# Chunk-selecting attention and a squared-ReLU feed-forward: the first four head pairs reordered, and their queries loaded in four transfers

## The chip, the cores and the metric

The kernel runs on one core of a Trainium2 chip. The core has a matrix engine (TensorE, PE in the profile, its weight loads PEld), a vector engine (VectorE, DVE), a scalar engine (ScalarE, ACT), a general one (GpSimd, POOL) and SyncE (SP), which here only issues transfers. Each engine works through its own instructions in the order in which they were written; semaphores tie the engines together. Transfers run on 16 DMA engines. The metric is device time in microseconds (us).

## The reference

What is computed, for 4 batches, 8 heads, 768 tokens and head dimension 64, and after it for 3072 tokens of width 512 with a hidden layer of 2048:

```python
k_chunks = k.reshape(B, H, nc, 32, D)
k_min, k_max = k_chunks.min(3), k_chunks.max(3)
ub = sum_d(maximum(q * k_min, q * k_max))        # a bound for each chunk of 32 keys
ub = where(causal, ub, -1e9)
top_chunks = argsort(ub)[..., -6:]
scores = q @ k.T / sqrt(D)
scores = where(chunk is in top_chunks and the key is not later than the query, scores, -1e9)
attn = softmax(scores)
x = (attn @ v)                                   # to B*S rows of H*D
h = relu(x @ w_in)
out = (h * h) @ w_out
```

## The kernel before

**Staging.** The work is cut into 32 slots, each a batch, a half of the sequence (384 queries) and a pair of heads; eight groups of four slots (`ORDER`), `s` counts slots and `NP` is 4. Slots 0 to 3 are the first half of batch 0, pairs 0 to 3. They are the start of the kernel, and the only slots with no feed-forward work beside them; from slot 4 on, units of the feed-forward of earlier groups are taken from a queue and stand between the attention's steps on TensorE.

**The order is written by hand** (`tc.manual_schedule()`): every engine's instructions stand in the order of the Python calls. For one slot these are the steps:

- `step_T` transposes k and q of the pair on TensorE (`tk`, `tq`), one after the other. In slots 0 to 3, q comes from the tile `qn0`, token by token, in three 128x128 transposes; k from the packed tile `kn`, in eight small ones. `step_P` picks the PSUM pools and calls it.
- `relus_T` makes the positive and negative part of q on ACT (`qr`); `extrema` makes chunk minima and maxima of k on DVE (`km`, two reductions) and spreads them (`kbd`). `step_T2` is both. `place` copies `tk` or `tq` to its place in `kqs`, on the engine it is given.
- `step_U` bounds the chunks (`ub`, TensorE), finds the eight largest of each row (`m`, DVE) and marks what is below the sixth; in slots 0 to 3 it writes the marks into columns of `qn0`.
- `step_V` transposes queries and marks together (`qt`) and copies them to `kqs` on DVE (L383; L393 and L394 from slot 4 on).
- `step_E(s, head, bank)` multiplies keys with queries (`ps`, three PSUM buffers) and takes the exponential on ACT (`e`). The one-hot codes of the keys' chunks in `kqs`, written by `codes`, add a large negative number for marked chunks. In bank 1 POOL cuts the diagonal with a select (L416).
- `step_F` multiplies with V (`po`), divides (`r`, `x`). `x_T` and `x_copy` transpose x for the feed-forward, whose first matmul is `ph` (L522).

`busy` issues small matmuls whose result nobody reads; they hold a PSUM buffer of the pool that they are given.

**Loads.** Pairs 0 and 1 of k and q come through `load_staged` on the queues of SP and ACT in float32 and are cast by `step_cast`. All other loads are POOL's, which converts on the way: first k of pairs 2 and 3 (`load_packed("k", 0, 4)`), then six loads of q of those pairs (`load_q0`: one for each block of 128 tokens and each head of a pair), then V (`load_vt`), and then those in `later`, which `go` issues. POOL's transfers use eight semaphores in turn: the ninth, the second of V, waits until the first has landed. SP issues, behind the staged loads, the one-hot codes of pairs 1 to 3 (`codes(0, 0, nc.sync.dma_start, 1, NP)`, L166, two transfers); those of pair 0 are copied by DVE.

**The front** is L618 to L674. In pair 0 and 1 it reads:

```python
    step_cast("k", 1)
    step_V(0)
    step_E(0, 0, 0)
    step_E(0, 0, 1)
    step_cast("q", 1)
    step_P(1)
    step_T2(1)
```

The loop that follows does slot s and prepares slot s + 2 (`step_P(s + 2)`, `relus_T`, `extrema`, L665 to L673), up to slot 5. Slot 4 begins at L698, before the first feed-forward units are pushed (L709). For slot 4, `step_P` uses the PSUM pool of the feed-forward (`ph`, two buffers) for k.

Of the kernel before, what the change touches and what calls it, by code (L numbers as in the profile page):

```python
# [16 lines left out]
HT = 3  # L17
HB = HT * 128
# [21 lines left out]
def kernel(  # L40
# [9 lines left out]
    nc = tc.nc  # L50
    B, H, S, D = q.shape
    NC = S // CH
    NT = S // 128
    NP = H // 2
# [17 lines left out]
    SROW = (0, D)  # L72
# [34 lines left out]
            in_=rows(n, *ORDER[g], 0, H)[:, 128 * j:128 * (j + 1)]  # L107
            .rearrange("h p d -> p h d"))

    def load_q0(j, h):  # L110
        nc.gpsimd.dma_start(
            out=qn0[:, j, 2:NP, 1 + h, :],
            in_=q[0, 4 + h:H:2, 128 * j:128 * (j + 1)].rearrange("h p d -> p h d"))

    def load_v(b, h0, h1):
        nc.gpsimd.dma_start(
# [3 lines left out]
    def load_vt(b, j):  # L120
        nc.gpsimd.dma_start(  # L121
            out=vn[b % 2][:, :, j, 0:D],
            in_=v[b, :, 128 * j:128 * (j + 1)].rearrange("h p d -> p h d"))
# [22 lines left out]
    ident = consts.tile([128, 128], BF16, tag="ident")  # L146
    make_identity(nc, ident)
    load_packed("k", 0, 4)
    for j in range(HT):
        for h in range(2):  # L150
            load_q0(j, h)
    for j in range(HT):
        load_vt(0, j)

    oneh = consts.tile([D, S], BF16, tag="oneh")
    nc.vector.tensor_scalar_mul(
# [3 lines left out]
    def codes(i, half, copy, p0=0, p1=NP):  # L160
        for h in range(2):
            copy(kqs[i][SROW[h]:SROW[h] + D, h, p0:p1, 2 * half, :],
                 oneh[:, HB * half:HB * half + HB].unsqueeze(1)
                 .to_broadcast([D, p1 - p0, HB]))

    codes(0, 0, nc.sync.dma_start, 1, NP)  # L166

    cmask = consts.tile([128, HT, 2, NC], BF16, tag="cmask", name="cmask")
    nc.vector.memset(cmask, 0.0)
# [40 lines left out]
    st = {}  # L210
# [18 lines left out]
    def step_cast(n, p):  # L229
        if n == "k":  # L230
            nc.vector.tensor_copy(packed("k", 0)[:, 2 * p:2 * p + 2], staged["k", p])
        else:
            nc.scalar.copy(qn0[:, :, p, 1:3, :], staged["q", p])

    def step_T(s, kp, qp):

        b, half, p = slots[s]
        t = st.setdefault(s, {})
        for n, (pool, tag) in zip("kq", (kp, qp)):
            x = t[n] = pool.tile([128, HB], BF16, tag=tag, name="t" + n)  # L240
            if n == "q" and s < NP:
                for j in range(HT):
                    nc.tensor.matmul(
                        x[:, 128 * j:128 * (j + 1)],
                        lhsT=qn0[:, j, p, 1:3, :].rearrange("p h d -> p (h d)"),
                        rhs=ident, is_transpose=True, start=True, stop=True)
                continue
            for hh in range(2):
                for j in range(TP):
                    nc.tensor.matmul(  # L250
                        x[D * hh:D * hh + D, PP * j:PP * j + PP],
                        lhsT=packed(n, s // NP)[:, 2 * p + hh, D * j:D * j + D],
                        rhs=ident[0:PP, 0:PP], is_transpose=True, start=True, stop=True)

    def step_T2(s):
        relus_T(s)
        extrema(st[s]["k"], s)
        if s >= NP:
            place(s, "k", nc.vector.tensor_copy)
            place(s, "q", nc.scalar.copy)  # L260

    def relus_T(s):
        b, half, p = slots[s]
        t = st[s]
        qr = t["qr"] = work.tile([128, 2, HB], BF16, tag="qr", bufs=3, name="qr")
        c = 128 * (1 - half)
        for w in range(2):
            o, i = qr[:, w, c:], t["q"][:, c:]
            if s >= NP:
                o, i = by_token(o), in_order(t["q"])[:, c // TP:, :]  # L270
            nc.scalar.activation(o, i, ACT.Relu, scale=(-1.0, 1.0)[w])

    def place(s, n, copy, h0=0, h1=2):
        b, half, p = slots[s]
        for h in range(h0, h1):
            copy(by_token(kqs[b % 2][QROW[h]:QROW[h] + D, h, p, 2 * half + "kq".index(n), :]),  # L276
                 in_order(st[s][n][D * h:D * h + D]))
# [58 lines left out]
    def step_P(s):  # L336
        if s // NP >= ON_PE:
            relus(s)
            return
        step_T(s, *((S_, Y) if s == NP + 1 else (F, Y) if s < NP + 2 else  # L340
                    (Y, S_) if s < 2 * NP + 1 else (S_, A)))
        if s >= NP + 2 and s != 2 * NP + 1:
            step_T2(s)
# [282 lines left out]
    step_P(0)  # L626
    busy(10)
    step_T2(0)
    place(0, "k", nc.scalar.copy)
    blank(1, NP, 3)  # L630
    step_U(0)
    busy(9)
    step_cast("k", 1)
    step_V(0)
    step_E(0, 0, 0)
    step_E(0, 0, 1)
    step_cast("q", 1)
    step_P(1)
    step_T2(1)
    for i in range(3):  # L640
        nc.vector.memset(nsel[i], 0.0)
    early.close()
# [1 line left out]
    for s in range(NP):  # L644
        last = s + 1 == NP
        if s:
            step_E(s, 0, 0)
            step_E(s, 0, 1)
        step_E(s, 1, 0)
        busy(8)  # L650
        step_U(s + 1)
        if last:
            place(s + 1, "k", nc.vector.tensor_copy, 0, 1)
        else:
            place(s + 1, "k", nc.scalar.copy)
        step_E(s, 1, 1)
        if last:
            place(s + 1, "k", nc.scalar.copy, 1, 2)
        if s:
            step_F(s - 1, 0)  # L660
            step_F(s - 1, 1)
        if last:
            x_T(0, 0, F)
        step_V(s + 1)
        step_P(s + 2)  # L665
        if last:
            x_copy(0, 0, 0, 2, nc.vector.tensor_copy)
            busy(10, *F)
        else:
            relus_T(s + 2)  # L670
            if s + 2 == NP:
                place(s + 2, "q", nc.scalar.copy)
            extrema(st[s + 2]["k"], s + 2)  # L673
        go(s, 99)  # L674
    parts = []

# [4 lines left out]
    for s, (b, half, p) in enumerate(slots):  # L681
        if s < NP:
            continue
        hb = s // NP
        nb = len(BANKS[half])
        hf = nb // 2
        quota = [((4, 4, 4, 4) if hb == 1 else (8, 6, 7, 7))[p]]
        for fn, *a in first.get(s, ()):
            fn(*a)
        if ON_PE - 1 <= hb < 2 * B - 1 and p == (2 if hb < ON_PE else 1):  # L690
            parts.extend(step_K(hb + 1))

        def f1():
            if quota[0] and queue:
                quota[0] -= 1
                fill(1, True)

        if s == NP:  # L698
            for n in range(hf):
                step_E(s, 0, n)  # L700
            step_F(s - 1, 0)
            step_F(s - 1, 1)
            relus_T(s + 1)
            x_T(0, 1, F, (0,))
            x_copy(0, 1, 0, 1, nc.vector.tensor_copy)
            busy(8, *A)
            x_T(0, 1, F, (1,))
            x_copy(0, 1, 1, 2, nc.vector.tensor_copy)
            push(0)  # L709
            extrema(st[s + 1]["k"], s + 1)  # L710
            place(s + 1, "k", nc.vector.tensor_copy)
            place(s + 1, "q", nc.scalar.copy)
        if s == 2 * NP:
            for n in range(hf):
                step_E(s, 0, n)
            relus_T(s + 1)
            place(s + 1, "q", nc.scalar.copy)
            x_T(1, 0, A)
            x_copy(1, 0, 0, 2, nc.vector.tensor_copy)
            step_F(s - 1, 0)  # L720
            step_F(s - 1, 1)
            f1()
            f1()
            x_T(1, 1, A)
            x_copy(1, 1, 0, 2, nc.scalar.copy)
            push(1)
            extrema(st[s + 1]["k"], s + 1)
            place(s + 1, "k", nc.vector.tensor_copy)
        if p == 0 and hb > 2:
            step_F(s - 1, 0)  # L730
            step_F(s - 1, 1)
            step_X(hb - 1, False)
        else:
            f1()
        if s > NP and s != 2 * NP:
            for n in range(hf):
                step_E(s, 0, n)
        k1()
        f1()
        if p == 0 and hb > 2:  # L740
            f1()
            f1()
        if hb > 1 and s != 2 * NP:
            f1()
        go(s, 2)
        for n in range(hf, nb):
            step_E(s, 0, n)
        if hb < ON_PE and p:
            k1()
        if s + 1 < NS:  # L750
            step_U(s + 1)
        f1()
        if p and s > NP:
            step_F(s - 1, 0)
            step_F(s - 1, 1)
        if half == 0:
            f1()
        if hb < ON_PE and p:
            k1()
        for n in range(hf):  # L760
            step_E(s, 1, n)
        f1()
        if s + 1 < NS:
            step_V(s + 1)
        k1()
        go(s, 99)
        for n in range(hf, nb):
            step_E(s, 1, n)
        k1()
        if s + 2 < NS:  # L770
            step_P(s + 2)
        f1()
        if half == 0:
            f1()
        while quota[0] and queue:
            f1()
# [38 lines left out]
```

## Time and profile before

| | us |
|---|---|
| median of 3 runs | 279.37 (278.88 to 279.73) |
| profiled execution, whole time | 278.57 |
| its span, first to last instruction | 276.9 |
| TensorE busy | 259.0 (94%) |
| ScalarE busy | 181.9 (66%) |
| VectorE busy | 168.8 (61%) |
| GpSimd busy | 92.1 (33%) |

The granted clock of TensorE is 1.000 over the whole span. A timeline row gives the start in us from the span's start, the length in us, the engine, the line, the operation with the tile it writes and what it reads, how many such instructions follow one another (x), and in brackets the idle time of the engine before it and what ended it. A row with x over 1 holds several instructions, which overlap a little. In the chain of waits a row is a start, a length and what the time went to. A row of the transfers gives the tile, the queue, the number, the size and the us from issue to landing.

### The profile page before, as it was taken

To read this page: it belongs to the slowest core of one execution; us is meant where nothing else is said; L and a number is where in the kernel's file an instruction comes from. 1 tells how busy PE (TensorE), PEld (TensorE's weight loads), DVE (VectorE), ACT (ScalarE), POOL (GpSimd) and SP (SyncE) were. 2 spreads that over 40 slices of the span, in tenths; PEclk is the share of its full clock that TensorE was granted. 3 is DMA by queue.
4 is the path that set the end of the run, shared out by engine and by line. 5 is a ranking of instruction groups with operands and counts; after the bars stand their busy time and mean duration, and the time that the engine had idled before them with its cause. 6 is when DMAs were issued, how large, how long until landed. Compare 5 with 4: busy or idle time off the path is not lost.

```text
span 276.9 us, 6716 instructions
## 1 busy us (share of the span) xinstructions
PE 259.0 (94%) x2497; PEld 163.3 (59%) x2497; DVE 168.8 (61%) x645; ACT 181.9 (66%) x400; POOL 92.1 (33%) x137
## 2 busy tenths in 40 slices
PE   7687898899999999999999999999999999999994
PEld 6466555556666566655565566745565566655543
DVE  6687999656994368635894378616883455413411
ACT  6798889588975787835675777825674777615500
POOL 8796356316532016521551116701121111000000
PEclk9999999999999999999999999999999999999999
DMA  7999999959999249998599459996423200111002
GB/s 132 142 204 212 182 214 208 138 66 139 156 182 146 71 115 151 123 162 151 115 143 129 114 104 141 127 130 163 101 63 59 76 2 0 40 39 40 38 38 76
DMA packets 98272, 32.05 MB, mean 116 GB/s; under 512 B 84640, under 2 KB 93984, under 8 KB 98240
## 3 DMA queue, kind: packets, MB, share of 16 engines
q0 software_dynamic: 64720, 14.42, 61.7%
q1 hardware_dynamic: 32432, 16.88, 28.8%
q10 hardware_dynamic: 1088, 0.33, 0.5%
q8 instruction: 19, 0.31, 0.5%
q14 instruction: 13, 0.11, 0.1%
HBM read 27.26 MB, written 6.29 MB: 121 GB/s over the span
## 4 chain that ended last, share of the span: by engine, by line
PE 68%; DVE 13%; DMA 8%; ACT 5%; issue 2%; POOL 1%; SPq 1%; ACTq 0%; POOLq 0%
PE py L538 25%; PE ph L522 22%; PE ps L407 9%; PE po L432 7%; DMA qn<-in_q_dram 3%; DMA kn<-in_k_dram 3%; DVE h L528 2%; ACT e L412 2%; DVE kq L276 2%; DMA xT<-x 1%; DVE km L319 1%; ACT ht L526 1%; SPq L482 1%; DVE x L442 1%; ACT ob L544 1%
## 5 line engine op out<-in xcount | busy, mean ns | idle before, releaser
L412 ACT ACTIVATE e<-ps 128x512 bf16<-128x512 f32 x192 | 96.8, 550 | 26.6 <-PE ps L407 26.5
L522 PE MATMUL ph<-xT,w_in 128*128 128x384 bf16 x512 | 99.2, 326 | 0.6 <-DMA xT<-x 0.3
L538 PE MATMUL py<-w_out,h 128*128 128x512 bf16 x368 | 88.5, 379 | 1.2 <-ACT ob L544 0.9
L526 ACT ACTIVATE ht<-ph 128x384 bf16<-128x384 f32 x128 | 62.6, 499 | 27.3 <-PE ph L522 25.7
L416 POOL TENSOR_SCALAR_AFFINE_SELECT e<-e 128x384 bf16<-128x384 bf16 x64 | 34.5, 543 | 137.5 <-ACT e L412 137.5
L528 DVE TENSOR_TENSOR h<-ht 128x384 bf16<-128x384 bf16 x128 | 46.3, 374 | 43.5 <-ACT ht L526 43.3
L522 PEld LDWEIGHTS <-w_in 128*128 128x128 bf16 x512 | 47.4, 97 | 30.3 <-issue 1.4
L407 PE MATMUL ps<-kq 128*128 128x384 bf16 (+2 forms) x320 | 56.4, 278 | 2.8 <-ACT e L412 1.2
L538 PEld LDWEIGHTS <-h 128*128 128x128 bf16 x368 | 34.9, 97 | 35.3 <-issue 1.7
L407 PEld LDWEIGHTS <-kq 128*128 128x128 bf16 x320 | 26.3, 97 | 14.4 <-issue 2.6
L432 PEld LDWEIGHTS <-e 128*128 128x128 bf16 x672 | 25.6, 98 | 7.3 <-issue 2.0
L361 DVE MAX8 m<-ub 128x8 f32<-128x24 f32 (+1 forms) x160 | 16.7, 171 | 20.6 <-PE ub L354 19.7
L432 PE MATMUL po<-vn,e 128*128 128x65 bf16 x672 | 26.9, 194 | 1.4 <-POOL e L416 0.8
L544 ACT COPY ob<-py 128x512 f32<-128x512 f32 x19 | 11.1, 585 | 22.7 <-PE py L538 22.3
L442 DVE TENSOR_TENSOR x<-po,r 128x384 bf16<-128x384 f32 x32 | 17.8, 557 | 1.1
L393 DVE COPY kq<-qt 64x384 bf16<-64x384 bf16 (+1 forms) x28 | 8.8, 315 | 12.4 <-PE qt L389 12.4
L105 POOL DMA_DIRECT2D kn<-in_k_dram x15 | 13.3, 888 | 0.2
L105 POOL DMA_DIRECT2D qn<-in_q_dram x15 | 13.3, 886 | 0.0
L319 DVE TENSOR_TENSOR km<-km 128x384 bf16<-128x384 bf16 (+3 forms) x40 | 11.5, 287 | 1.1
L121 POOL DMA_DIRECT2D vn<-in_v_dram x12 | 10.7, 903 | 2.0 <-DVE kq L383 1.5
L354 PE MATMUL ub<-kbd,qr 128*128 128x48 bf16 (+1 forms) x160 | 9.6, 180 | 1.9 <-DVE kbd L218 1.0
L354 PEld LDWEIGHTS <-qr 128*128 128x128 bf16 x160 | 7.7, 96 | 4.2 <-ACT kq L276 1.3
(67 smaller groups left out, 198.8 us busy)
## 6 DMA issues: line engine op xcount, KB each, us to landing
out_dram<-ob SPq DMA_DIRECT2D x23, 256.0 KB, 2.2
kq<-kqT SPq DMA_DIRECT2D x10, 384.0 KB, 5.2
w_in<-in_moe_w_in_dram POOLq DMA_DIRECT2D x2, 1024.0 KB, 13.2
w_out<-in_moe_w_out_dram POOLq DMA_DIRECT2D x2, 1024.0 KB, 18.2
kn<-in_k_dram POOLq DMA_DIRECT2D x15, 128.0 KB, 6.0
qn<-in_q_dram POOLq DMA_DIRECT2D x15, 128.0 KB, 5.9
vn<-in_v_dram POOLq DMA_DIRECT2D x12, 128.0 KB, 9.2
vn<-in_v_dram POOLq DMA_DIRECT2D x4, 384.0 KB, 8.2
```

The source lines that it names most:

```text
L105: nc.gpsimd.dma_start(out=nat_of(n, g)[:, DM * j:DM * j + DM].rearrange("p (h d) -> p h d", d=D), in_=rows(n, *ORDER[g], 0, H)[:, 128 * j: ...
L354: nc.tensor.matmul(ub[:, j - j0], lhsT=st[s]["qr"][:, w, 128 * j:128 * (j + 1)], rhs=kbds[b % 2][:, p, w, :, 0:ncs], start=False, stop=(j ...
L361: nc.vector.max(out=m8[:, j, hh, :], in_=ub[:, j - j0, hh, :])
L407: nc.tensor.matmul(ps[:, at:at + 128 * m], lhsT=kqs[b % 2][:, hh, p, 2 * (j // HT), 128 * (j % HT):128 * (j % HT + 1)], rhs=qc(s, hh)[:, c ...
L412: nc.scalar.activation(e[:, 512 * n + lo:512 * n + hi], ps[:, lo:hi], ACT.Exp, scale=float(scale))
L416: nc.gpsimd.affine_select(out=d, in_=d, compare_op=ALU.is_ge, fill=0.0, base=0, channel_multiplier=-1, pattern=[[0, 3], [1, 128]])
L432: nc.tensor.matmul(po[:, hh, i, :], lhsT=t["e"][hh][:, c:c + 128], rhs=vn[b % 2][:, 2 * p + hh, j, :], start=(j == 0), stop=(j == iq))
L442: nc.vector.tensor_mul(x[:, :, 128 * p:128 * (p + 1)].rearrange("p j (h d) -> p h j d", h=2), po[:, :, :, 0:D], r.to_broadcast([128, 2, HT ...
L522: nc.tensor.matmul(ph[:, 0:HB], lhsT=w_in[:, ki, 128 * f:128 * (f + 1)], rhs=xT[:, ki, :], start=(ki == 0), stop=(ki == NKI - 1))
L526: nc.scalar.activation(ht, ph[:, 0:HB], ACT.Relu)
L528: nc.vector.tensor_mul(h, ht, ht)
L538: nc.tensor.matmul(py[t], lhsT=h2[hb, f][:, 128 * t:128 * (t + 1)], rhs=w_out[:, f, :], start=(f == 0), stop=(f == NFI - 1))
```

## The change

The queries of pairs 2 and 3 are loaded by head, each load with all 384 tokens: heads 4 and 5 before V, heads 6 and 7 after it. The codes of pairs 1 to 3 are issued later in SP's queue: two one-element memsets on DVE, behind the extrema of pair 0, write into the region that the codes then overwrite, so SP waits for them. The cast of pair 1's q stands before pair 0's scores, its k transposes before them, its q transposes after their first bank, its extrema on DVE after its relus are issued. `step_T` gets an argument that selects k or q. Slot 4 is prepared in slot 3, after the scores of its first head, instead of at the end of slot 2, and the copies of its q come after the last exponential of slot 3; slot 5 is prepared in slot 4, after `step_F` of slot 3.

```diff
-    def load_q0(j, h):
+    def load_q0(h):
         nc.gpsimd.dma_start(
-            out=qn0[:, j, 2:NP, 1 + h, :],
-            in_=q[0, 4 + h:H:2, 128 * j:128 * (j + 1)].rearrange("h p d -> p h d"))
+            out=qn0[:, :, h // 2, 1 + h % 2, :],
+            in_=q[0, h, 0:HB].rearrange("(j p) d -> p j d", p=128))
...
     load_packed("k", 0, 4)
-    for j in range(HT):
-        for h in range(2):
-            load_q0(j, h)
+    for h in (4, 5):
+        load_q0(h)
     for j in range(HT):
         load_vt(0, j)
+    for h in (6, 7):
+        load_q0(h)
...
-    codes(0, 0, nc.sync.dma_start, 1, NP)
...
-    def step_T(s, kp, qp):
+    def step_T(s, kp, qp, ns="kq"):
...
-        for n, (pool, tag) in zip("kq", (kp, qp)):
+        for n in ns:
+            pool, tag = kp if n == "k" else qp
...
     step_T2(0)
+    for h in range(2):
+
+        nc.vector.memset(kqs[0][SROW[h]:SROW[h] + D, h, 1, 0, 0:1], 0.0)
+    codes(0, 0, nc.sync.dma_start, 1, NP)
     place(0, "k", nc.scalar.copy)
...
     step_cast("k", 1)
+    step_cast("q", 1)
     step_V(0)
+    step_T(1, F, Y, "k")
     step_E(0, 0, 0)
+    step_T(1, F, Y, "q")
+    relus_T(1)
     step_E(0, 0, 1)
-    step_cast("q", 1)
-    step_P(1)
-    step_T2(1)
+    extrema(st[1]["k"], 1)
...
             step_E(s, 0, 1)
+        if last:
+            step_P(s + 1)
+            relus_T(s + 1)
+            extrema(st[s + 1]["k"], s + 1)
         step_E(s, 1, 0)
...
         if last:
+            place(s + 1, "q", nc.scalar.copy)
             place(s + 1, "k", nc.scalar.copy, 1, 2)
...
         step_V(s + 1)
-        step_P(s + 2)
         if last:
             x_copy(0, 0, 0, 2, nc.vector.tensor_copy)
             busy(10, *F)
-        else:
-            relus_T(s + 2)
-            if s + 2 == NP:
-                place(s + 2, "q", nc.scalar.copy)
-            extrema(st[s + 2]["k"], s + 2)
+        elif s + 2 < NP:
+            step_P(s + 2)
+            step_T2(s + 2)
         go(s, 99)
...
             step_F(s - 1, 1)
+            step_P(s + 1)
             relus_T(s + 1)
```

## The prediction

> **What bounds the kernel now.** I read the page's head and chain by engine first, then the chain of waits of the first 32 us in order of time, then the timelines of the front, engine by engine.
>
> ```profile
> span 276.9 us, 6716 instructions
> PE 68%; DVE 13%; DMA 8%; ACT 5%; issue 2%; POOL 1%; SPq 1%; ACTq 0%; POOLq 0%
> ```
>
> Two thirds of the chain is TensorE at work that the diff leaves alone. What can be won lies before TensorE has feed-forward work to fill its waits, that is before the first `ph` matmul.
>
> ```profile
> 1.56 6.93 DMA kn<-in_k_dram
> ...
> 11.53 8.50 DMA qn<-in_q_dram
> ...
> 20.07 0.37 PE tq L250 x8
> ...
> 21.18 0.47 ACT kq L276
> ...
> 22.16 0.61 ACT e L412
> ...
> 27.17 0.36 DVE xT L472
> ```
>
> The chain up to the first `ph` (27.22) is POOL's loads until 20.03, where the packed queries of group 1 land, then the transpose of pair 4, its placing on ACT, the four exponentials of pair 3 behind that, and the transposition of x. So two things must both get shorter for the front to gain: the road of pairs 0 to 3, and what hangs on that landing.
>
> Timeline of the front (start, length, engine, line, tile):
>
> ```profile
> 2.27 0.46 SPq L135 DMA_DIRECT2D stage<-in_q_dram  x1
> 2.37 4.23 POOL L111 DMA_DIRECT2D qn<-in_q_dram  x6
> 2.77 1.36 SPq L162 DMA_DIRECT2D kq<-oneh  x2
> 7.22 0.68 ACT L189 ACTIVATE qn<-ident 128x576 bf16<-128x576 bf16 x1
> 8.54 0.49 PE L407 MATMUL ps<-kq 128*128 128x384 bf16 x3 [0.65 <-DVE kq L383]
> 8.96 0.87 ACT L412 ACTIVATE e<-ps 128x512 bf16<-128x512 f32 x2 [1.05 <-PE ps L407]
> 8.96 0.37 PE L250 MATMUL tk<-ident,kn 96*64 96x96 bf16 x8
> 9.03 1.75 POOL L121 DMA_DIRECT2D vn<-in_v_dram  x2 [1.52 <-DVE kq L383]
> 9.38 0.56 DVE L216 TENSOR_REDUCE km<-tk 128x12 bf16<-128x384 bf16 x1 [0.90 <-PE tk L250]
> 9.71 0.51 ACT L233 CAST qn<-stage 128x384 bf16<-128x384 f32 x1
> 10.44 0.18 DVE L218 TENSOR_TENSOR kbd<-hmask,km 128x48 bf16<-128x48 bf16 x1
> 10.66 0.66 ACT L271 ACTIVATE qr<-tq 128x256 bf16<-128x256 bf16 x2 [0.43 <-PE tq L243]
> 10.61 0.63 DVE L641 MEMSET nsel<- 128x192 uint32 x3
> 11.65 0.41 DVE L361 MAX8 m<-ub 128x8 f32<-128x12 f32 x4 [0.40 <-PE ub L354]
> 13.53 0.70 PE L407 MATMUL ps<-kq 128*128 128x384 bf16 x5
> ```
>
> ACT is idle from 7.90 (7.22 + 0.68) to 8.96, does two exponentials of pair 0, and only then casts the queries of pair 1. On that cast hang its transposes, the relus at 10.66, the maxima at 11.65 and the scores of pair 1 at 13.53. From there each pair takes 3.30 us (13.53 to the end of pair 3's copy, 19.53 + 0.55 in the rows further down, and 0.05, for two pairs).
>
> **The change part by part.**
>
> *Cast of pair 1 ahead of the exponentials.* It can start at 7.90 for ACT, but its data comes later:
>
> ```profile
> stage<-in_q_dram SPq DMA_DIRECT2D x1, 96.0 KB, 6.4
> ...
> kq<-oneh SPq DMA_DIRECT2D x1, 144.0 KB, 6.7
> ```
>
> The later half of the stage was issued at 2.27 and took 6.4, so it lands at 8.7. Cast 8.78 to 9.29, transposes until 9.69 (now relus start 0.44 after the cast's end; the first exponential fits between), relus at about 9.79 instead of 10.66: 0.87 earlier. The key side is no later: the transposes of k move ahead of pair 0's scores, into the 0.65 that TensorE waits before 8.54, and the minima start when DVE ends the copy at 8.49 instead of at 9.38. `kbd` then ends near 9.65 (1.24 after the start, as 9.38 to 10.62 now), the three memsets of nsel (0.63) near 10.28, and the maxima start at 10.78, set by the relus. Bounds: nothing, if the cast's data came when the cast runs now; 1.37 if it were there at once (the memsets at 10.28 then set the maxima). I take 0.87: the stage stands ahead of the one-hot codes in SP's queue before and after, so its landing should not move.
>
> *One-hot codes behind two tiny memsets and `kbd` of pair 0.* SP issues them at about 6.4 and 7.1 instead of 2.77 and 3.5. Now they land 6.7 after issue, at 9.5 and 10.3, just behind the stage at 8.7, so nearly all of that is queueing. With the queue's front unchanged I expect 9.5 to 11. Scores of pair 1 need them at 12.66 (13.53 less 0.87). Bounds: no cost; or 6.7 after the later issue, 13.8, which would hold those scores until 13.85. SP holds nothing else behind them before the first output. The memsets fit between `kbd` and the maxima of pair 0, on an idle DVE.
>
> *Four query loads for six.* By heads each has 384 rows instead of 256, so the bytes and the 128-byte pieces stay 1536; six issues cost 4.23, four at the 0.82 of the first k load at most 3.3. With only four, all three V loads go out without waiting for a semaphore's return (now 9.03, behind kn's landing at 8.49), then the last two queries, by about 8. The packed loads of group 1 follow kn's landing at about 9.0 and 9.8 instead of 10.76 and 11.53. The queue that now runs thin then stays filled:
>
> ```profile
> DMA packets 2809, 0.39 MB, mean 97 GB/s; under 512 B 2760, under 2 KB 2808, under 8 KB 2808
> ...
> DMA packets 2602, 0.36 MB, mean 158 GB/s; under 512 B 2555, under 2 KB 2591, under 8 KB 2602
> ```
>
> These are two stretches of nothing but small pieces: 9.8 to 13.8 at 97, 29.8 to 32.1 at 158. At the later rate the first would be 1.5 us shorter. I let all later landings move ahead by 1.2 (bounds 0 and 1.75, the earlier issue), so group 1's queries land near 18.8. The queries of pair 3 come behind V; by issue at 7.3 plus the 6.9 of the kn load they land by 14.2, and their transposes stand just ahead of pair 2's scores (13.53 + 3.30 − 0.87 = 15.96), so they cost nothing. The second and third V load are issued some 4 earlier than now, their reader moves by 0.87: nothing either.
>
> *Pair 4 moved behind pair 3's first scores.* The last pairs now:
>
> ```profile
> 14.44 0.18 DVE L218 TENSOR_TENSOR kbd<-hmask,km 128x48 bf16<-128x48 bf16 x1
> 14.78 0.27 PE L407 MATMUL ps<-kq 128*128 128x256 bf16 x1
> 19.53 0.55 DVE L383 COPY kq<-qt 128x768 bf16<-128x768 bf16 x1
> 19.79 0.38 ACT L412 ACTIVATE e<-ps 128x256 bf16<-128x256 f32 x1
> 20.50 0.66 ACT L271 ACTIVATE qr<-tq 128x256 bf16<-128x256 bf16 x2 [0.33 <-PE tq L250]
> 23.82 0.47 ACT L276 COPY kq<-tk 64x384 bf16<-64x384 bf16 x1
> 24.35 0.72 PE L616 MATMUL idle<-ident 128*128 128x128 bf16 x10
> 24.91 0.38 PE L407 MATMUL ps<-kq 128*128 128x384 bf16 x2
> 25.50 0.33 PE L466 MATMUL pt<-ident,x 128*128 128x128 bf16 x3
> ```
>
> Call T the end of pair 3's copy, 20.08 now and 19.21 after. Now the scores of pair 4 start at T + 4.83. After: scores of pair 3 at T + 0.05, pair 4's k transposes 0.42 later and its minima another 0.42 (8.54, 8.96, 9.38 above), `kbd` ready after 1.24: T + 2.13. The last scores of pair 3 follow 0.16 behind a `kbd` (14.62 to 14.78) and take 0.27; exponential 0.38; then ACT places q (0.96) and the second half of k (0.47), where the exponentials used to come last. That ends at T + 4.4. The ten fillers need the PSUM buffer which this frees, and the scores of pair 4 start 0.56 after them (24.35 to 24.91): T + 5.03. So 0.20 is lost again. The eight exponentials and copies are the same, only reordered. With T = 19.21 the scores of pair 4 start at 24.24, 0.67 before now. The transposes of pair 5 (two sets of the 0.37 above, overlapping: 0.52, up to 24.35) no longer hide in ACT's time but stand between the AV product of pair 3 and the x transposes; these end 1.44 after the scores instead of 0.92, and DVE takes x up 1.50 after them anyway. I charge 0.05. First `ph`: about 0.6 earlier, at 26.6; the first half of w_in lands earlier too. Bounds of this part: a loss of 0.3 more, if pair 5's 0.52 showed by half, or nothing lost.
>
> *What comes after `ph`.* Until 49 us the chain is DVE almost without a break, then TensorE; both move rigidly. One place does not:
>
> ```profile
> vn<-in_v_dram POOLq DMA_DIRECT2D x1, 128.0 KB, 14.7
> ...
> 32.51 0.90 POOL L567 DMA_DIRECT2D w_out<-in_moe_w_out_dram  x1 [0.48 <-ACT qr L271]
> 33.42 1.00 POOL L416 TENSOR_SCALAR_AFFINE_SELECT e<-e 128x384 bf16<-128x384 bf16 x2
> 33.17 0.83 DVE L218 TENSOR_TENSOR kbd<-hmask,km 128x48 bf16<-128x48 bf16 x1
> ```
>
> This `kbd` takes 0.83 where others take 0.18, and ends with POOL's first select. The selects stand behind the w_out issue, which waits for the V load issued at 17.53 (14.7: lands 32.23). If that load comes 1.2 earlier, the first select ends near 32.75, and `kbd`, wanted at 32.57, ends near 32.8 instead of 33.4 by the shift alone. Bounds 0 and 0.65; I take 0.4, since the second select may still step in.
>
> [...]
>
> *Sum* against the profiled execution (278.57, of which 276.9 is the span): −0.87 + 0.20 + 0.05 − 0.40 = −1.0, or 277.5. The median of the runs shown is 279.37, 0.8 above it; the same difference gives 278.4.
>
> **The rivals.**
>
> *Only the front moves.* The landings after w_in move no more than the front, and the long `kbd` stays long: −0.6, 278.8. For it: w_in's 2 MB set the pace there. Against it: the thin stretch at 97 GB/s.
>
> *It does not do what it says.* Pair 4's later start, its placing behind four exponentials and pair 5's transposes eat the 0.87 (0.20 + 0.05 + 0.3, and DVE's copies of pair 4 another 0.3): 279.4. For it: the chain at 20 us was held by ACT, which does the same amount as before.
>
> *Larger.* The staged queries land sooner, with the codes out of SP's queue, and the maxima start at 10.28; with the whole 0.65 of `kbd`: −1.37 + 0.25 − 0.65, 277.6. Against it: the codes stood behind them.
>
> *Slower: the codes come late.* They now compete with a queue of V and query pieces that has no gap. At 6.7 from issue (13.8) pair 1's scores are 0.3 late; at the 8.5 which the query load of group 1 took in such a queue, 15.6, they are 2.1 late. With the 0.25 lost behind and the `kbd` half relieved, that is 279.7 to 281.5, say 280.6. It decides from a landing of about 12.7 on, and makes the kernel slower than before from 13.4 on (13.45 − 13.53 + 0.25 − 0.2 = 0). Against it: the landing just behind the stage.
>
> **How the numbers follow.** A measurement of this kernel can tell about 0.3%, 0.84 us, from no change. Chances: the forecast 0.40, only the front 0.20, nothing 0.13, larger 0.13, codes late 0.14. The forecast's size is uncertain by 0.4, so of its 0.40 I count 0.29 as faster than 278.53 and 0.11 as the same; of "only the front" 0.05 and 0.15; "larger" is all faster, "nothing" 0.12 same and 0.01 slower, "codes late" 0.11 slower and 0.03 same. Together 0.47 faster, 0.41 same, 0.12 slower. The likeliest alone: 278.0 to 278.9. The range reaches from the larger case to half way into the late codes: 277.4 to 280.0.
>
> **What would show it.** The cast of pair 1 at 8.8 and the relus near 9.8; codes landed before 11.5 and the scores of pair 1 near 12.65 without a wait for a DMA; pair 3's copy ending near 19.2; no wait for group 1's queries in the chain; the fillers before pair 4's scores waiting for ACT's last placing, at 23.6; first `ph` at 26.6; the `kbd` after 32 us at 0.2 to 0.4. Wrong if a DMA of the codes heads the chain at 13 us, if the cast still waits past 9, or if the first `ph` stays at 27.

## The result, and the profile after

Over 22 executions of each on one chip, the changed kernel took 279.82 us in the median (278.12 to 282.37) and the kernel before 279.05 (277.88 to 279.91): a ratio of 1.0032, 95% interval 1.0016 to 1.0048. The slowest execution of the changed kernel, 282.37, counts as slow and is left out of the ratio. So the change makes the kernel slower, by 0.8 us, where 1.0 less was forecast.

The profiled execution of the changed kernel took 282.07 us, one of the slowest of its 22, so what it shows is read piece by piece and not by its total. The page's head and its chain by engine:

```profile
span 280.3 us, 6689 instructions
PE 69%; DVE 13%; ACT 6%; DMA 6%; issue 3%; SPq 1%; POOL 1%; ACTq 0%; POOLq 0%
```

The engines' shares hardly tell anything. The chain of waits of the first 32 us does (start, length, what the time went to):

```profile
6.36 0.00 DVE kq L631
...
6.41 7.45 DMA kq<-oneh
13.86 0.14 issue
14.00 0.60 PE ps L407 x3
...
29.03 0.36 DVE xT L472
```

Before, this stretch belonged to POOL's loads of k and q. Now it begins with the tiny memset of `kqs` at L631, and the next 7.45 us are the transfer of the one-hot codes, which lands at 13.86. The timeline of the same execution answers to the prediction's steps:

```profile
3.86 2.66 POOL L121 DMA_DIRECT2D vn<-in_v_dram  x3
6.41 1.35 SPq L163 DMA_DIRECT2D kq<-oneh  x2
6.49 1.50 POOL L111 DMA_DIRECT2D qn<-in_q_dram  x2
8.17 0.51 ACT L232 CAST qn<-stage 128x384 bf16<-128x384 f32 x1 [0.19 <-DMA stage<-in_q_dram]
8.95 0.38 PE L407 MATMUL ps<-kq 128*128 128x384 bf16 x2 [0.28 <-DVE kq L383]
9.17 0.33 PE L243 MATMUL tq<-ident,qn 128*128 128x128 bf16 x3
9.86 0.66 ACT L271 ACTIVATE qr<-tq 128x256 bf16<-128x256 bf16 x2
10.85 0.41 DVE L361 MAX8 m<-ub 128x8 f32<-128x12 f32 x4 [0.18 <-PE ub L354]
12.12 0.56 DVE L383 COPY kq<-qt 128x768 bf16<-128x768 bf16 x1 [0.55 <-PE qt L378]
14.00 1.29 PE L407 MATMUL ps<-kq 128*128 128x384 bf16 x5 [1.34 <-DMA kq<-oneh]
18.50 0.71 PE L407 MATMUL ps<-kq 128*128 128x384 bf16 x5
21.19 0.55 DVE L383 COPY kq<-qt 128x768 bf16<-128x768 bf16 x1
26.14 0.72 PE L616 MATMUL idle<-ident 128*128 128x128 bf16 x10 [0.92 <-ACT kq L276]
26.70 0.38 PE L407 MATMUL ps<-kq 128*128 128x384 bf16 x2
28.99 1.46 PE L522 MATMUL ph<-xT,w_in 128*128 128x384 bf16 x8
35.36 0.18 DVE L217 TENSOR_TENSOR kbd<-hmask,km 128x48 bf16<-128x48 bf16 x1
```

The front gained what it should up to 12.7: relus of pair 1 at 9.86, maxima at 10.85, the marked queries in place at 12.68. There TensorE stops and waits 1.34 for the codes. Pair 1's scores come at 14.00 instead of 13.53 before. The next step is the second loss: from pair 1's to pair 2's scores it takes 4.50 (14.00 to 18.50) where a pair took 3.30. The windows show why (length, then the busy us of PE, PEld, DVE, ACT and POOL with the number of instructions, then the granted clock, the DMA share and GB/s). First the changed kernel, then the kernel before:

```profile
10.81:14.23 3.42, 1.44 (x21) 0.89 (x19) 2.29 (x9) 2.46 (x6) 1.96 (x4) 1.00 1.55 179
14.23:17.65 3.42, 3.32 (x37) 2.68 (x35) 1.04 (x7) 2.80 (x6) 2.68 (x5) 0.50 1.44 213
17.65:21.06 3.41, 3.04 (x50) 2.41 (x49) 2.97 (x12) 2.53 (x7) 3.41 (x5) 1.00 1.05 194
```

```profile
7.83:11.25 3.42, 1.82 (x28) 1.31 (x25) 2.38 (x7) 1.93 (x7) 2.22 (x3) 1.00 1.82 154
```

In the changed kernel TensorE was busy for 1.44 of 3.42 us up to 14.23, and for the next 3.42 us it got half its clock. Five score matmuls took 1.29 where that stretch begins, and 0.71 at 18.50, behind its end. In the profiled execution of the kernel before, no half-clock window stands in the front. By the first `ph`, 28.99 against 27.22, 1.77 us were lost.

The rest of this execution's excess came later, and no other profile shows it. Its chain has this row:

```profile
124.07 7.26 DMA xT<-x
```

The transposition of x by DMA landed at 131.3, and TensorE waited 2.5 for it; in the kernel before it landed at 127.2, and in the ten experiments between 125.9 and 128.8.

### The profile page after: what moved, and what is told of

Its sections match the earlier page's. It is cut to its first block, busy times and chain, and to the rows that moved or that the text cites. A ratio compares the mean times of both kernels' runs of the same rounds, so it can differ in the third digit from the quotient of the medians.

```text
span 280.3 us, 6689 instructions
## 1 busy us (share of the span) xinstructions
PE 259.8 (93%) x2472; PEld 165.7 (59%) x2497; DVE 168.6 (60%) x647; ACT 182.1 (65%) x400; POOL 91.0 (32%) x135
## 4 chain that ended last, share of the span: by engine, by line
PE 69%; DVE 13%; ACT 6%; DMA 6%; issue 3%; SPq 1%; POOL 1%; ACTq 0%; POOLq 0%
PE py L538 25%; PE ph L522 22%; PE ps L407 10%; PE po L432 7%; DMA kq<-oneh 3%; DMA xT<-x 3%; ACT e L412 3%; DVE h L528 2%; PE idle L616 2%; DVE kq L276 2%; DVE km L319 1%; ACT ht L526 1%; DVE x L442 1%; DVE km L215 1%; ACT ob L544 1%
## 5 line engine op out<-in xcount | busy, mean ns | idle before, releaser
L538 PE MATMUL py<-w_out,h 128*128 128x512 bf16 x343 | 83.9, 379 | 2.6 <-ACT ob L544 0.9
L407 PE MATMUL ps<-kq 128*128 128x384 bf16 (+2 forms) x320 | 57.1, 279 | 3.3 <-DMA kq<-oneh 1.3
L616 PE MATMUL idle<-ident 128*128 128x128 bf16 x97 | 9.6, 268 | 2.3 <-POOL ident masks.py:199 1.4
```

Of the source, the lines that this page charges most:

```text
L407: nc.tensor.matmul(ps[:, at:at + 128 * m], lhsT=kqs[b % 2][:, hh, p, 2 * (j // HT), 128 * (j % HT):128 * (j % HT + 1)], rhs=qc(s, hh)[:, c ...
L538: nc.tensor.matmul(py[t], lhsT=h2[hb, f][:, 128 * t:128 * (t + 1)], rhs=w_out[:, f, :], start=(f == 0), stop=(f == NFI - 1))
L616: nc.tensor.matmul(idle, lhsT=ident, rhs=ident, start=True, stop=True)
```

## Where the codes were

The view of the transfers, us 8 to 9, gives each queue's packets, MB and time as a share of 16 engines. q0 carries POOL's transfers, q1 SP's. In the changed kernel:

```profile
DMA packets 1225, 0.15 MB, mean 154 GB/s; under 512 B 1225, under 2 KB 1225, under 8 KB 1225
...
q0 software_dynamic: 1225, 0.15, 242.2%
```

SP had issued the codes at 6.41 and 7.17, and in this microsecond not one of its packets moved. The first codes' pieces (768 bytes) come at 9.69. Issued early, as in the kernel before, the codes stood among the first transfers; issued at 6.4 they find all three V loads (issued 3.86 to 6.52) and three loads of k and q in POOL's queue.

## The experiments

All were timed with five rounds, 12 executions of each beside 23 to 35 of the kernel before on the same chip (e9 and e10 on another chip than e1 to e8, so the ratios compare better than the medians). Each gave these, with times in us from the span's start for the last three columns (profiled execution):

| | median | ratio to before, 95% | codes land | pair 1's scores | first `ph` |
|---|---|---|---|---|---|
| before | 278.93 to 279.30 | | 9.46, 10.26 | 13.53 | 27.22 |
| after | 279.82 | 1.0032 [1.0016, 1.0048] | 13.86, 14.56 | 14.00 | 28.99 |
| e1 codes early | 279.21 | 0.9992 [0.9965, 1.0019] | 10.24, 11.57 | 13.25 | 29.05 |
| e2 only codes late | 278.55 | 0.9994 [0.9972, 1.0016] | 10.64, 11.91 | 13.53 | 27.23 |
| e3 six loads | 278.38 | 0.9977 [0.9956, 0.9999] | 9.60, 11.47 | 12.45 | 26.95 |
| e4 fillers in the wait | 279.44 | 1.0018 [0.9996, 1.0039] | 14.05, 15.04 | 14.19 | 28.50 |
| e5 codes by engines | 278.15 | 0.9970 [0.9943, 0.9997] | none for pair 1 | 12.62 | 26.45 |
| e6 queries, then V | 278.15 | 0.9981 [0.9955, 1.0007] | 12.53, 13.40 | 12.67 | 27.25 |
| e7 codes in two parts | 278.68 | 0.9986 [0.9963, 1.0008] | 14.10, 14.84 | 14.23 | 29.16 |
| e8 only the loads | 279.23 | 1.0005 [0.9983, 1.0027] | 10.35, 11.58 | 13.74 | 29.08 |
| e9 before, codes by engines | 279.89 | 1.0024 [1.0008, 1.0040] | none for pair 1 | 15.31 | 29.32 |
| e10 e5 with six loads | 278.60 | 0.9985 [0.9958, 1.0012] | none for pair 1 | 12.84 | 26.93 |

**e1: the changed kernel, codes issued at their old place.**

```diff
+    codes(0, 0, nc.sync.dma_start, 1, NP)
     cmask = consts.tile([128, HT, 2, NC], BF16, tag="cmask", name="cmask")
...
-    for h in range(2):
-
-        nc.vector.memset(kqs[0][SROW[h]:SROW[h] + D, h, 1, 0, 0:1], 0.0)
-    codes(0, 0, nc.sync.dma_start, 1, NP)
```

> The changed kernel, with the one-hot codes issued at their old place and the two small memsets gone; all else as changed. Theory (the late codes and the clock they cost are the loss): the codes land near 9.5 and 10.3 again, no transfer holds the scores of pair 1, which start near 12.7 (14.0 in the changed kernel), the clock stays at 1.0 from the start on, the first ph comes near 26.6, and the time is 0.6 to 1.2 us below the kernel before. Rival 1 (the reordering of pairs 3 to 5 or the loads cost by themselves): the first ph stays at 28 or later and the time stays within 0.3 us of the changed kernel. Rival 2 (the staged queries of pair 1 need the queue to themselves): they land 0.6 later than the 8.09 of the changed kernel, so the scores of pair 1 start at 12.7 instead of 12.1; the gain is then at the lower end.

The time came back to that of before and no further. Two rows of its timeline say why:

```profile
9.92 0.34 PE L245 MATMUL tq<-ident,qn 128*128 128x128 bf16 x3 [0.79 <-ACT qn L234]
...
22.08 0.54 PE L252 MATMUL tq<-ident,qn 96*64 96x96 bf16 x8 [1.01 <-DMA qn<-in_q_dram]
```

With the codes among the early transfers, the stage landed at 9.28 instead of 8.09 and group 1's queries at 22.04 instead of 19.27. TensorE waited for these, and its windows show the same sequel as in the changed kernel, later:

```profile
18.62:22.04 3.42, 1.55 (x25) 0.94 (x21) 2.45 (x9) 2.40 (x6) 2.62 (x4) 1.00 1.19 166
22.04:25.45 3.41, 3.37 (x42) 3.02 (x43) 1.46 (x8) 2.18 (x6) 2.60 (x5) 0.50 1.12 211
```

So the early place of the codes only moved the loss from one transfer to another, as long as the new loads filled POOL's queue.

**e2: the kernel before, only the codes late; e3: the changed kernel with the old six query loads, all ahead of V.** In e2 the memsets and `codes` stand behind `step_T2(0)` as in the change, and nothing else is changed. In e3:

```diff
-    for h in (4, 5):
-        load_q0(h)
+    for j in range(HT):
+        for h in range(2):
+            load_q0(j, h)
     for j in range(HT):
         load_vt(0, j)
-    for h in (6, 7):
-        load_q0(h)
```

> The kernel before, with nothing changed but the place of the codes: behind the two memsets, as in the changed kernel. Theory: the codes are issued at 6.4 and join a queue of small pieces that is already full; they land between 12 and 14. The scores of pair 1, at 13.53 in the kernel before, wait 0 to 0.5 for them; the time is 0 to 1 us above the kernel before, more if the clock falls. If the codes land near 10 here, it is not the late issue alone but V ahead of them that makes them late. Rival (the codes are harmless): time and scores as in the kernel before, or better, since the staged queries land sooner.

> The changed kernel with the six old query loads ahead of V; the order of everything else as changed. It tells the loads from the front. Theory: the codes wait behind what POOL's queue already holds; with the second and third V load issued only at 9, that queue runs empty near 11.5, and the codes land at 11.5 to 13, 1 to 2 us sooner than the 13.86 of the changed kernel; the scores of pair 1 start at 12.6 to 13.1, the clock does not fall, and the time is 0.3 to 1 us below the kernel before. Rival (the late issue alone decides): codes land at 13.9 as in the changed kernel, and the time is as there.

From issue to landing the codes took 7.4 us in the changed kernel (median of the two, by the view of the transfers of the first 17 us). The same row of e2, and then of e3 (number, size, us):

```profile
kq<-oneh SPq DMA_DIRECT2D x2, 144.0 KB, 4.5
```

```profile
kq<-oneh SPq DMA_DIRECT2D x2, 144.0 KB, 3.7
```

Issued at the same late moment, the codes land by 12 in both, and nobody waits. In e2 both queues move in us 8 to 9, where in the changed kernel only POOL's did:

```profile
q0 software_dynamic: 444, 0.05, 84.8%
q1 hardware_dynamic: 165, 0.11, 48.2%
```

The late issue alone is harmless; it needs V ahead of it to hurt. e3 keeps the whole reordered front, and is faster than the kernel before, by an interval that ends just below 1. What it lacks is V in time:

```profile
14.74 0.38 PE L431 MATMUL po<-vn,e 128*128 128x65 bf16 x7 [0.59 <-DMA vn<-in_v_dram]
```

**e4: the changed kernel with 20 fillers in the wait.**

```diff
             step_P(s + 2)
             step_T2(s + 2)
+        if s == 0:
+            busy(20)
         go(s, 99)
```

> The changed kernel with 20 filler matmuls more on TensorE between the transposes of pair 2 and the scores of pair 1, that is into the wait for the codes. The wait stays, TensorE is busy in it. Theory: the scores of pair 1 still start at 14.0, but the clock does not fall to half for 3.4 us, so pairs 1 to 3 keep their 3.30 us each, and the time is 0.5 to 1 us below the changed kernel. Rival (the fall of the clock costs nothing, since DVE and ACT set the pace there): time and first ph as in the changed kernel.

All 12 executions had a mean clock of at least 0.997, against 2 of 22 of the changed kernel, and the window up to 14.23 now reads:

```profile
10.81:14.23 3.42, 2.45 (x42) 1.91 (x40) 2.29 (x9) 2.55 (x7) 1.86 (x4) 1.00 1.64 169
14.23:17.65 3.42, 2.67 (x46) 2.04 (x47) 1.43 (x8) 2.80 (x6) 2.50 (x4) 1.00 1.41 216
```

From pair 1's to pair 2's scores it takes 3.83 instead of 4.50, and the first `ph` comes 0.5 earlier. So by the profile the clock is part of the loss. By time alone this is not shown: the median is 0.4 lower, short of the 0.5 to 1 that was expected, and the two intervals overlap. What is left at full clock is the larger part: e4's 12 executions have a median of 279.44, and the nine of the kernel before beside them that also had a mean clock of at least 0.997 have 278.64. That difference holds the wait and whatever the fillers cost.

**e5: the changed kernel, pair 1's codes written by the engines.** Head 0 by DVE behind pair 0's `kbd`, head 1 by ACT behind the cast of pair 1's queries; only pairs 2 and 3 are left to SP.

```diff
-    def codes(i, half, copy, p0=0, p1=NP):
-        for h in range(2):
+    def codes(i, half, copy, p0=0, p1=NP, hs=(0, 1)):
+        for h in hs:
...
-        nc.vector.memset(kqs[0][SROW[h]:SROW[h] + D, h, 1, 0, 0:1], 0.0)
-    codes(0, 0, nc.sync.dma_start, 1, NP)
+        nc.vector.memset(kqs[0][SROW[h]:SROW[h] + D, h, 2, 0, 0:1], 0.0)
+    codes(0, 0, nc.sync.dma_start, 2, NP)
+    codes(0, 0, nc.vector.tensor_copy, 1, 2, (0,))
...
     step_cast("q", 1)
+    codes(0, 0, nc.scalar.copy, 1, 2, (1,))
```

> The changed kernel, with the codes of pair 1 copied by DVE (head 0, behind the first kbd) and ACT (head 1, behind the cast of pair 1), as those of pair 0 are; the transfers carry pairs 2 and 3 alone, at the changed kernel's place. Theory (the late codes are the whole loss, and V ahead of the last queries is a gain of its own): the scores of pair 1 start at 12.7 to 13.1 without a wait, those of pair 2 at 16 to 16.5, since V has landed before its first reader (in the run with six loads that reader waited 0.59 for V and pair 2 came at 16.46), first ph at 26.3 to 26.7, the clock stays up, and the time is 0.8 to 1.3 us below the kernel before, and below the run with six loads. Rival (the four loads slow something else): time at or above the run with six loads.

Its timeline has the prediction's course:

```profile
9.76 0.65 ACT L271 ACTIVATE qr<-tq 128x256 bf16<-128x256 bf16 x2
...
12.62 0.71 PE L407 MATMUL ps<-kq 128*128 128x384 bf16 x5
...
18.66 0.55 DVE L383 COPY kq<-qt 128x768 bf16<-128x768 bf16 x1
...
23.61 0.72 PE L616 MATMUL idle<-ident 128*128 128x128 bf16 x10 [0.93 <-ACT kq L276]
...
24.16 0.38 PE L407 MATMUL ps<-kq 128*128 128x384 bf16 x2
...
32.49 0.61 DVE L217 TENSOR_TENSOR kbd<-hmask,km 128x48 bf16<-128x48 bf16 x1
```

Scores of pair 1 at 12.62 (12.66 was forecast), pair 3's copy ending at 19.21 (19.21), pair 4's scores at 24.16 (24.24), first `ph` at 26.45 (26.6). It is faster than both kernels: 0.8 us below the kernel before, ratio 0.9970. That it is faster than e3 is not shown, since their intervals overlap; the profiles show only that pair 2's scores come at 15.92, without e3's wait for V, where e3 has 16.46.

**e6: the changed kernel, queries of heads 4 to 7 all ahead of V; e7: the changed kernel, pair 1's codes as transfers of their own.**

```diff
-    for h in (4, 5):
+    for h in (4, 5, 6, 7):
         load_q0(h)
...
-    for h in (6, 7):
-        load_q0(h)
```

```diff
-    codes(0, 0, nc.sync.dma_start, 1, NP)
+    codes(0, 0, nc.sync.dma_start, 1, 2)
+    codes(0, 0, nc.sync.dma_start, 2, NP)
```

> The changed kernel, with all four query loads ahead of V. It tells the number of the loads from the place of V. Theory (codes wait as long as POOL's queue is full without a gap): POOL issues V from 5.4 on, so that V's pieces follow the queries' without a gap, and the codes still land late, at 12.5 to 14; the scores of pair 1 wait and the time is as in the changed kernel, within 0.4. Rival (it is V ahead of the last queries that holds the codes): the codes land at 10 to 11.5 as with six loads, and the time is below the kernel before by 0.3 to 1.

> The changed kernel, with the codes of pair 1 as two transfers of their own, ahead of those of pairs 2 and 3. Theory: the first piece of the codes still comes only near 9.5, but a third of the pieces is through by 11.7 to 12.3, in time for the scores of pair 1 at 12.7; the clock stays up, and the time is that of the run in which DVE and ACT write these codes, within 0.3. Rival (the landing is set by what POOL has queued, not by the size): the first two transfers land at 13 or later, the scores of pair 1 wait, and the time stays within 0.4 of the changed kernel.

```profile
13.54 0.38 PE L405 MATMUL ps<-kq 128*128 128x384 bf16 x2 [0.38 <-DMA kq<-oneh]
```

```profile
14.23 0.49 PE L407 MATMUL ps<-kq 128*128 128x384 bf16 x3 [1.68 <-DMA kq<-oneh]
```

In e6 (first row) V is issued behind two more loads and the codes land in between, 12.53 and 13.40; the wait shrinks to 0.38. The landing is what the theory said, the time rather what the rival said, though its interval includes 1. So V's place counts. The number of the query loads is not cleared by this: with six of them (e3) the codes landed at 9.60 and 11.47, and POOL issued the second load of V only at 7.81, where e6 issued all of V from 5.37 to 8.03. In e7 (second row) a third of the bytes landed no sooner, at 14.10, though their first pieces moved at 8.80, so the size of the codes' own transfer does not set the landing. The time contradicts the rival all the same: e7's ratio, 0.9986 [0.9963, 1.0008], lies below that of the changed kernel, 1.0032 [1.0016, 1.0048]. Its profiled execution, 279.76, is the slowest of its 12 and 1.1 above their median, so by what the split helps is not seen and stays open.

**e8: the kernel before with the new loads alone.** `load_q0` and its order as in the diff of the change, nothing else.

> The kernel before with nothing changed but the query loads: four by heads, the last two behind V. Theory: the codes are ahead in SP's queue and land near 10 as before; V lands near 13 but its first reader comes at 14.9 anyway; pair 1 is still held by its cast. The scores start as in the kernel before, and the time is within 0.3 us of it. Rival (the loads by heads are slow by themselves, as one run with early codes may hint, in which the first k load landed 0.5 later than before and the packed queries 2.0 later): the packed queries of group 1 land after 21, TensorE waits for them, and the time is 0.5 or more above.

No gain, the time that the theory said, but with the wait that the rival said: like e1, TensorE waited for group 1's queries, which landed at 21.50 against 20.03 before:

```profile
21.55 0.48 PE L251 MATMUL tq<-ident,qn 96*64 96x96 bf16 x8 [1.42 <-DMA qn<-in_q_dram]
```

The loads by themselves bring nothing.

**e9: the kernel before with pair 1's codes by the engines; e10: e5 with the six loads ahead of V.** e9 has the edits of e5 on the kernel before, with ACT's copy ahead of `step_cast("q", 1)` and SP's transfers of pairs 2 and 3 at their old place. The loads of e10 are those of e3.

> The kernel before, with the codes of pair 1 written by the vector engine (head 0) and the scalar engine (head 1) as in e5; those of pairs 2 and 3 stay in SP's queue at their old place. If the gain of e5 comes from the reordered front and the loads, and the codes only had to be out of their way, this kernel is no faster than before: pair 1's scores near 13.5, first ph at 27.2 or a little later (the scalar engine has 0.4 more to do before the cast of pair 1), ratio 0.999 to 1.002. Rival: writing the codes by engines is itself the gain; then the ratio comes near the 0.997 of e5 and the first ph lies before 26.8.

> e5 with the six query loads of before, all ahead of V. With the codes out of the way of both orders, what is left between this and e5 is the number and order of the loads. If V behind six loads costs what e3 showed, a wait for V near 16 us of about 0.6, the first ph is at 26.9 and the ratio 0.998 to 0.999. Rival: the order is worth nothing once the codes are by engines, first ph at 26.5, ratio as e5, 0.997. In neither case is there a stretch of half clock in the front.

e9 is slower than the kernel before, so having the engines write the codes is, at these places, no gain in itself. It is also slower than expected, 1.0024 where 0.999 to 1.002 was said, and two views show it:

```profile
11.16 0.50 PE L243 MATMUL tq<-ident,qn 128*128 128x128 bf16 x3 [1.63 <-ACT qn L233]
```

```profile
6.83:10.24 3.41, 2.00 (x26) 1.24 (x25) 2.15 (x9) 2.12 (x5) 2.39 (x3) 1.00 1.84 176
10.24:13.65 3.41, 2.25 (x20) 1.71 (x20) 1.74 (x10) 2.75 (x7) 2.11 (x4) 0.50 1.49 98
```

The codes on ACT put off the cast, TensorE waited 1.63, and the clock was halved for 6.83 us, to 17.07. That none of its 12 executions reached a mean clock of 0.997 says that this is no accident of one. e10 came out as expected in size, first `ph` at 26.93, 0.48 after e5's, with no half clock in the front, but not in cause. TensorE did not wait for V. The stage landed at 8.33 for e5's 8.05, so that all of pairs 1 to 3 is 0.2 to 0.3 late, and pair 4's `kbd` took 0.37 for 0.18. In time the two cannot be told apart, as their intervals overlap.

## Why the prediction was wrong

**The step that failed** is "One-hot codes behind two tiny memsets": "With the queue's front unchanged I expect 9.5 to 11." Measured were 13.86 and 14.56. The argument looked at SP's queue alone, where nothing had changed ahead of the codes. What had changed was the other queue: by 6.52 POOL had issued all of V, an effect that the prediction itself listed under the loads and used only for its gain. e2 and e3 show that the same late issue lands by 12 without V ahead of it, e6 that moving V behind two more queries takes the wait from 1.34 to 0.38, and e5 that the rest holds once pair 1's codes are no transfer.

**The rival "the codes come late"** named this mechanism, with 13.8 as the lower end of the landing and 279.7 for it, and got a chance of 0.14. The argument against it, "the landing just behind the stage", was no argument: that landing belonged to an issue at 2.77, when POOL had issued one load of k and one of q. The price is near the measured 279.82 by luck, since the sum behind it is not what happened, and that 279.82 lies within the stated 277.4 to 280.0 is owed to this rival. From the changed kernel to e5 the first `ph` differs by 2.54 us. Of these, 1.38 is the later score of pair 1 (14.00 and 12.62), and 1.20 the longer way to pair 2's scores (4.50 instead of 3.30) at half clock, which no case of the prediction had; 0.04 is regained by the first `ph`. In the medians that 2.54 is worth about 1.7 (279.82 and 278.15); where the rest is regained was not followed.

**Cast of pair 1.** Right. Relus at 9.86, and 9.76 in e5, for 9.79. The stage landed at 8.09, sooner than the 8.7 taken, as the "larger" rival had it, and it was worth nothing: the transposes at 9.17 stand on TensorE behind pair 0's first scores at 8.95. The working has a slip that changed nothing: 1.24 after 8.49 is 9.73 and not 9.65, so the bound of 1.37 should have been 1.29.

**Four loads for six.** Half right. V was issued without a wait, and group 1's queries came 0.8 sooner (19.27 against 20.03; 18.53 in e5, for the 18.8 forecast). That this was a gain without a price was wrong: with POOL's queue filled without a gap, others came late, the codes (13.86), or the queries of group 1 if the codes go first (22.04 in e1, 21.50 in e8).

**Pair 4 behind pair 3's first scores.** Right. From T to pair 4's scores it took 4.96 in the changed kernel (21.74 to 26.70) and 4.95 in e5, where 5.03 was forecast, and the ten fillers wait for ACT's last placing as said.

**The long `kbd`.** The sizes are uncertain. In the changed kernel it took 0.18 at 35.36, but that stretch has moved by over 2 us against POOL's selects. In e5, where all else came as forecast, it took 0.61, a relief of 0.22 for the 0.4 that was taken; in the other experiments it took 0.18 to 0.67. That POOL's selects make it long was the author's reading of its end beside the first of them before (34.00); it was not tried by itself. Pair 1's `kbd` kept its 0.18 in the changed kernel (at 9.86), but took 0.53 in e2, at 10.44, beside a V issue from 8.97 to 10.73. Beside the same issue the kernel before has 0.18, so what decides is not shown.

**The sum.** With the codes out of the way, e5's profiled execution took 276.99 against 278.57, and its median is 0.78 below that of the kernel before. So the forecast's −1.0 comes near what e5 did, not what the changed kernel did.

**What stays open** is why the codes' pieces did not move until 9.69, where in e2, issued at 6.36, the first one moved at 7.73. An order of issue over both queues would about fit the landings above; it was not tried by itself and is not shown.

## What to carry to other kernels

In the changed kernel a transfer that was issued later (6.41 for 2.77) landed behind what another queue had issued meanwhile: the codes at 13.86 for 9.46, behind three loads of V issued by 6.52 that took 7.0 in the median. So a landing must be worked out from all queues; that nothing changed in the transfer's own queue did not keep it in time here (13.86 for 9.5 to 11). When a change fills the gap in one queue, look for what was living in the gap. Small constants that a tight path waits for can be cheaper on an engine with a spare half microsecond than in a transfer, provided that engine is not the one that the path hangs on: so it was in e5 (ratio 0.9970, where the change has 1.0032) and was not in e9 (1.0024).

## What was unexpected of the hardware

The prediction had no change of clock in it. In the changed kernel TensorE's clock was halved after a wait of 1.34 us, for 3.41 us (14.23 to 17.65), and in e9 for 6.83, twice that (10.24 to 17.07). Lay the profiles out in steps of these 3.41 us, counted from the clock's changes: a half-clock window followed a window with 1.44 of 3.42 us busy (changed kernel), 1.55 (e1), and this one of e7:

```profile
11.77:15.18 3.41, 1.47 (x20) 0.83 (x18) 1.67 (x4) 1.98 (x6) 2.49 (x4) 1.00 1.56 184
```

e8 has two windows that were busy for almost the same time. After the first the clock stayed whole, after the second it was halved:

```profile
8.01:11.42 3.41, 1.72 (x26) 1.29 (x25) 2.48 (x8) 1.82 (x6) 2.13 (x3) 1.00 2.83 169
18.25:21.67 3.42, 1.76 (x39) 1.32 (x38) 2.88 (x12) 2.10 (x6) 3.19 (x5) 1.00 1.18 183
```

At 1.82 (the kernel before, 7.83 to 11.25, in steps from 4.42, where its record of the clock begins) the clock stayed whole, and so it did in the changed kernel over its longest wait, 2.5 us before 131.5, which fell across two windows:

```profile
126.86:130.27 3.41, 2.12 (x13) 0.91 (x11) 1.26 (x4) 1.56 (x3) 0.61 (x1) 1.00 1.93 143
130.27:133.69 3.42, 2.22 (x15) 1.40 (x16) 0.83 (x2) 1.36 (x3) 0.00 (x0) 1.00 0.92 241
```

So in these traces the clock went with the busy time within a window rather than with the length of a wait (1.34 halved, 2.5 not): in the fronts shown here it was halved after all windows of 1.55 and less, and between 1.72 and 2.00 it went either way, e9 with 2.00 of 3.41 being halved. What decides in between is not shown. That the kernel before has a window at 1.82, within that stretch, would explain why two thirds to three quarters of its executions (22 of 34, 17 of 23, 26 of 35) also show a mean clock below 0.997; this is argued, not shown, since only one of them has a trace. Ahead of the first record of the clock (7.41 in the changed kernel) the views give 1.00 although nothing is on record there: the ten fillers at 5.50 took 1.27, those of the kernel before at 5.43 took 0.72.
